# Two GpSimd subtractions made to wait for VectorE's in a tuned attention and mixture kernel

## The chip, the cores and the metric

The kernel runs on one core of a Trainium2 chip. The metric is the device time of one execution in microseconds (us), the median of three runs. Engines are called as the profile calls them: PE is TensorE's matmul, PEld its weight load, DVE is VectorE, ACT is ScalarE, POOL is GpSimd, SP is SyncE.

## What is computed

Attention with a sliding window of 128 positions, then a mixture of four two-layer experts that are all applied to every token, in float32:

```python
# attention: B, H, S, D = 4, 8, 576, 64
scores = q @ k.T / sqrt(D) - slope[h] * (i - j)       # only 0 <= i - j < 128
attn   = softmax(scores) @ v
# experts: N = 2304 tokens, D = 512, E = 4, F = 1024
p = domain_probs / (domain_probs.sum(-1, keepdims=True) + 1e-09)
for e in range(E):
    h = np.maximum(x @ w1[e], 0.0)
    out += p[:, e:e + 1] * (h @ w2[e])
```

## The kernel before

Every float32 operand of a matmul is split into a high part (a cast to the PE's rounded type) and a low part (the operand minus its high part), and a product takes three matmuls: high by high, high by low, low by high. So wherever a matrix is made, a cast (mostly ACT, L338) and a subtraction (DVE or POOL, `minus`, L355) come behind it. On POOL a subtraction or sum over 384 columns or more is cut in two pieces (`pieces`, L346), which leaves two instructions.

The Python program doesn't write its instructions down in a fixed order. It collects operations (`Plan.op`, L55) with the engines that can run them, what they read and write, and a due time. `Plan.order` (L88) then goes forward in estimated time, and at each step takes for an engine the ready operation with the earliest due time. It keeps an account called `port`, which lets no two operations of DVE and POOL that carry that mark overlap in its own estimate. The instructions go out in the order of their planned starts. What keeps the engines apart on the chip are semaphores for true data dependencies alone: the account of `port` leaves no trace in the program.

The last 200 us of the span are six "pairs" (`pair`, L1329). A pair takes two slices of 256 hidden features of one expert together with the last 768 tokens, and multiplies in Strassen's manner with seven products in place of eight, in both layers. Its first layer is products `("a", 0..6)` and `("b", 0..6)` (L1236), its second the seven products of `multiply` (L1459; matmuls at L1469), whose results DVE weights and adds to the accumulators (`weighted`, L1487; instructions at L1488). The left operands of four of the second layer's products are sums of first-layer results, called S1 to S4. Each exists for fi = 0 and 1. For S2 and S3, for example:

- the raw S3 is made by DVE into a tile `q` (L1384), the raw S2 by `plus` from it into a tile `w1r` (L1431, instructions at L1090), the raw S4 by `plus` from that into a tile `q` (L1432, instructions at L1090)
- `split(i, fi)` (L1396) makes the high part on ACT (L338) and the low part by `minus` (L360). For S1 and S2 the subtraction may only go to DVE; in the trace these are the rows `xl<-w1r,xh`. For S3 and S4 it may go to either engine; S3's are on POOL in the trace, `rl<-q,rh`, two pieces of 128x192 for each fi.

The products of one pair that use S2 (`2`), S3 (`3`), "22" and S4 (`4`) are worked off between the first-layer products of the next pair, in the order a0, 2 (tiles 0 and 1), a1, 2 (tile 2), a2, 3 (tiles 0 and 1), and so on (L1339). Product 2 adds to the PSUM bank that product 11 of its own pair has just filled, so its first matmul has to wait until DVE has read that bank at L1488.

Before, L1433 to L1436 read:

```python
                split(3, fi)
                if fi:
                    split(2, 0)
                    split(2, 1)
```

Of the kernel before, what the change touches and what calls it, by code (L numbers as in the profile page):

```python
# [12 lines left out]
ALU = mybir.AluOpType  # L13
# [4 lines left out]
PE, DVE, ACT, POOL, SP = "PE", "DVE", "ACT", "POOL", "SP"  # L18


def f(ap):
    return ap.bitcast(F32)
# [13 lines left out]


class Op:
    __slots__ = ("n", "engs", "emit", "due", "deps", "outs", "wait", "ready", "bufs", "cold", "start", "end", "eng", "port", "late", "lag")


class Plan:
# [9 lines left out]
    def __init__(self):  # L52
        self.ops, self.last, self.readers, self.places = [], {}, {}, {}

    def op(self, engs, emit, due, reads=(), writes=(), holds=(), cold=None, port=None, late=0.0, lag=0.0):  # L55

        o = Op()
        o.n, o.engs, o.emit, o.due = len(self.ops), dict(engs), emit, due
        o.deps, o.outs, o.bufs, o.start = set(), [], [], None


        o.port, o.late, o.lag = (POOL,) if port is None else port, late, lag
        o.cold = 2 * o.engs.get(PE, 0.0) if cold is None else cold
        for key in reads:
            if key in self.last:
                o.deps.add(self.last[key])
        for key in writes:
            if key in self.last:
                o.deps.add(self.last[key])
            o.deps.update(self.readers.get(key, ()))  # L70
        o.deps.discard(o)
        for key in reads:
            self.readers.setdefault(key, []).append(o)
        for key in writes:
            self.last[key] = o
            self.readers[key] = []
        for key in (*reads, *writes, *holds):
            b = key[0] if isinstance(key, tuple) else key
            b = getattr(b, "buf", b)
            if isinstance(b, Buf) and b not in o.bufs:  # L80
                o.bufs.append(b)
                b.uses += 1
        for d in o.deps:
            d.outs.append(o)
        self.ops.append(o)
        return o
# [153 lines left out]
def key_of(b):  # L240
    return b.key if isinstance(b, Part) else b
# [3 lines left out]
def attention_moe(  # L245
# [28 lines left out]
    plan = Plan()  # L274
# [47 lines left out]
    after = sb.tile([P, 2, P], F32, tag="after", name="after")  # L322
# [5 lines left out]
    by = {DVE: nc.vector, POOL: nc.gpsimd}  # L328
# [4 lines left out]
    def cast(o, i, n, due, reads, writes, sbuf=True):  # L333


        def emit(e):
            if e == ACT:
                nc.scalar.activation(o(), i(), AF.Copy)  # L338
            else:
                nc.vector.tensor_copy(o(), i())  # L340

        plan.op(
            {ACT: act(n) + (0.035 if sbuf else 0.0), DVE: dve2(n) if sbuf else dve(n)}, emit, due, reads, writes, port=(DVE,) if sbuf else ()
        )

    def pieces(e, n, *aps):  # L346

        if e != POOL or n < WHOLE:
            return [aps]
        axis = next((i for i in range(1, len(aps[0].shape) - 1) if aps[0].shape[i] % 2 == 0), len(aps[0].shape) - 1)  # L350
        m = aps[0].shape[axis] // 2
        at_ = (slice(None),) * axis
        return [[x[(*at_, slice(i * m, i * m + m))] for x in aps] for i in range(2)]

    def minus(o, a, b, n, due, reads, writes, gp=True):  # L355


        def emit(e):
            for x, y, z in pieces(e, n, o(), a(), b()):
                by[e].tensor_tensor(out=x, in0=y, in1=f(z), op=ALU.subtract)  # L360

        engs = {DVE: dve(n), POOL: pooled(n)} if gp else {DVE: dve(n)}
        plan.op(engs, emit, due, reads, writes, port=(DVE, POOL) if gp else ())

    a, b = EARLY
# [10 lines left out]
    for us, nbs in passes:  # L378
        for u in us:
# [3 lines left out]
            if max(nbs) <= PAIRED and u % 2 == 0 and u + 1 in us:  # L383
                half_of[l], half_of[l + 1] = 0, 1
                for nb in nbs:
                    n = BLOCKS[nb][1]
# [26 lines left out]
            for nb in nbs:  # L413
                n = BLOCKS[nb][1]
# [20 lines left out]
    end = opened[5]  # L435
    if SEVEN[3, 4] < NU:
        end = next(now for l, nb, now in steps if nb == (3, 4)) - AHEAD
# [39 lines left out]
    def segment(g):  # L477
# [59 lines left out]
        if g.plain:  # L537
            return
        cast(lambda: g.kh[:, :, :kn], lambda: k[:, :, :kn], 2 * kn, due, [k], [g.kh])
        cast(lambda: g.qs[:, :, :n], lambda: q[:, :, :n], 2 * n, due, [q], [g.qs])  # L540
        minus(
            lambda: g.qs[hi64, :, :n],
            lambda: q[hi64, :, :n],
# [4 lines left out]
            [g.qs],  # L548
        )
        minus(  # L550
            lambda: g.kl[:, :, :kn],
            lambda: k[:, :, :kn],
# [7 lines left out]
        due += 3  # L560
        cast(lambda: g.vs[:, :vn, 0:4:3, :], v4, 128 * vn, due, [v], [(g.vs, 0)])
        minus(
            lambda: g.vs[:, :vn, 1:3, :],
            v4,
# [449 lines left out]
    def after_group(n0):  # L1014
        for o in plan.ops[n0:]:
            for d in gate:
                if d not in o.deps:
                    o.deps.add(d)
                    d.outs.append(o)
# [67 lines left out]
    def plus(o, a, b, n, due, reads, writes, op=ALU.add):  # L1087
        def emit(e):
            for x, y, z in pieces(e, n, o(), a(), b()):
                by[e].tensor_tensor(out=x, in0=y, in1=z, op=op)  # L1090

        plan.op({DVE: dve(n), POOL: pooled(n)}, emit, due, reads, writes, port=(DVE, POOL))
# [236 lines left out]
    def pair(l0, l1, due, between):  # L1329
# [3 lines left out]
        n = BLOCKS[nbs[0]][1]  # L1333
# [11 lines left out]
        ready, t_ = {}, clock[0]  # L1345
        for x in order:
            x = x if isinstance(x, tuple) else (None, x.__defaults__[-1])
# [20 lines left out]
        for fi in range(2):  # L1368
            h, lo = Buf("rh"), Buf("rl")
# [8 lines left out]
        def relu(o, src, reads, k_, d):  # L1378
            plan.op({ACT: act(n)}, lambda e: nc.scalar.activation(o(), src(), AF.Relu), d, reads, [k_])

        def joined(o, src, b, op, reads, k_, d, sbuf):
            plan.op(
                {DVE: dve(n)},
                lambda e: nc.vector.scalar_tensor_tensor(out=o(), in0=src(), scalar=0.0, in1=f(b()), op0=ALU.max, op1=op),  # L1384
                d,
                reads,
                [k_],
                port=(DVE,) if sbuf else None,
            )

        def halves(name, fi, src, keys, d, sbuf, free=()):
            h, lo, hk, lk = R[name, fi]
            relu(h, src, [*keys, *free], hk, d)
            joined(lo, src, h, ALU.subtract, [*keys, hk], lk, d, sbuf)

        def split(i, fi):  # L1396
            h, lo, hk, lk = S[i, fi]
            r_, rk = s_raw(i, fi), s_key(i, fi)
            n0 = len(plan.ops)
            cast(h, r_, n, ready[i], [rk], [hk])  # L1400
            minus(lo, r_, h, n, ready[i], [rk, hk], [lk], i > 2)
            if i < 3:
                after_group(n0)

# [12 lines left out]
        def result1(src, keys, fi, b):  # L1417
            d = clock[0] - URGENT
            if b == 0:
                h, lo = (Part(t, lambda t: t[:, fi, n : 2 * n], ("r", fi)) for t in (xh, xl))  # L1420
                R["11", fi] = (lambda: h[:, :n]), (lambda: lo[:, :n]), key_of(h), key_of(lo)
                hold.append((src, keys, fi, d))
            else:
                joined(s_raw(1, fi), src, raw(a22, fi), add, [*keys, key(a22, fi)], s_key(1, fi), d - 3, fi == 1)
                relu(raw(a21, fi), src, keys, key(a21, fi), d)
                split(1, fi)
            if len(hold) == 1 and (b == 1) == (fi == 0):
                src, keys, fi, d = hold.pop()
                halves("11", fi, src, keys, d, False, free)
                joined(s_raw(3, fi), src, raw(a21, fi), sub, [*keys, key(a21, fi)], s_key(3, fi), d, False)  # L1430
                plus(s_raw(2, fi), s_raw(3, fi), raw(a22, fi), n, ready[2] - 0.5, [key(a22, fi), s_key(3, fi)], [s_key(2, fi)], sub)  # L1431
                plus(s_raw(4, fi), raw(a12, fi), s_raw(2, fi), n, ready[4] - 0.5, [key(a12, fi), s_key(2, fi)], [s_key(4, fi)])  # L1432
                split(3, fi)  # L1433
                if fi:
                    split(2, 0)
                    split(2, 1)  # L1436

        spare = Buf("av")
        s0, at0, _ = sevenfold(l0, due, result0, Part(spare, lambda t: t.place[0], 0))
# [193 lines left out]
    for i in range(FILL):  # L1633
# [5 lines left out]
            out=after,  # L1639
# [19 lines left out]
            out=dps, in0=dps, scalar1=1.0e-9, scalar2=None, op0=ALU.add  # L1659
# [9 lines left out]
            out=prob, in0=dp, in1=dps[:, :, None].to_broadcast([P, NT // P, E]), op=ALU.mult  # L1669
# [18 lines left out]
    outs = []  # L1688
    for l, nb, due in [*steps, (None, None, now)]:
# [35 lines left out]
        if l is not None:  # L1725
            outs = [] if l in pairs else [(l, b, i) for b in (nb if l in joint else [nb]) for i in range(BLOCKS[b][1] // P)]

    with tc.manual_schedule():
        for o in plan.order():
            o.emit(o.eng)  # L1730


MARGIN = 15.32
# [65 lines left out]
```

## Time and profile before

| | us |
|---|---|
| median of three runs | 911.28 (911.26 to 913.27) |
| the profiled execution, its own time | 911.12 |
| its span in the trace | 909.1 |
| PE busy | 883.8 (97%) |
| DVE busy | 739.5 (81%) |
| POOL busy | 462.0 (51%) |

The profile covers one execution. An engine's line of a timeline gives the start, the duration, and in square brackets how long the engine had been idle and what released it. A duration runs from the start of an instruction on its engine to its end, and so holds any time in which it stood still there. "x3" merges neighbours of one kind into one row, which then runs from the first start to the last end. Times in the trace count from the start of the span.

### The profile page before, as it was taken

The page shows a single profiled execution, that of the slowest core. Times are in us where ns is not written, and L with a number is a line of the kernel's source. Part 1 is how long each engine was busy: PE and PEld are TensorE (multiplying, and loading weights), DVE is VectorE, ACT ScalarE, POOL GpSimd, SP SyncE. Part 2 cuts the span into 40 slices and gives each one's busy share as a digit, 9 for nine tenths or more (in the row PEclk, how much of TensorE's full clock was granted, in tenths as well). Part 3 has the DMA queues.
Part 4 walks back from the last instruction along what each step waited for, and adds up shares of the span by engine and source line. Part 5 has one row for each costly group of instructions (what it writes and reads, how often), then busy time and mean ns, then how long its engine had stood idle before and what let it go on. Part 6 is the DMA issues. An engine that isn't in the chain of part 4 may idle for free.

```text
span 909.1 us, 15674 instructions
## 1 busy us (share of the span) xinstructions
PE 883.8 (97%) x5466; PEld 816.2 (90%) x5466; DVE 739.5 (81%) x1605; ACT 474.6 (52%) x1221; POOL 462.0 (51%) x595
## 2 busy tenths in 40 slices
PE   8999999999999999999999999999999898998997
PEld 5899999999999999999998989899998898998997
DVE  6989879888887889886998878778665879879877
ACT  6877456565677678663443534334242533543542
POOL 4787555556457678763672213218314415535524
PEclk9999999999999999999999999999999999999999
DMA  7766554242445456432366464642333533533602
GB/s 239 228 199 194 170 169 134 86 153 85 136 164 157 141 179 217 139 120 65 128 242 245 163 218 148 215 150 76 110 96 137 186 105 112 201 105 111 203 1 70
DMA packets 47999, 136.19 MB, mean 150 GB/s; under 512 B 4656, under 2 KB 19760, under 8 KB 44848
## 3 DMA queue, kind: packets, MB, share of 16 engines
q1 hardware_dynamic: 43696, 113.17, 37.7%
q0 software_dynamic: 4224, 22.02, 7.2%
q8 instruction: 43, 0.70, 0.3%
q14 instruction: 36, 0.29, 0.1%
HBM read 106.86 MB, written 28.31 MB: 149 GB/s over the span
## 4 chain that ended last, share of the span: by engine, by line
PE 84%; DVE 10%; DMA 2%; ACT 2%; issue 1%; SPq 1%; DVEq 0%; ACTq 0%
PE b L1564 29%; PE b L1158 19%; PE b L1236 18%; PE b L1469 8%; PE av L819 4%; PE b L609 3%; DVE acc L1488 2%; PE b L746 2%; DMA w2r<-in_w 1%; DVE acc L1582 1%; PE av L1469 1%; DVE xl L360 1%; DVE w2l L360 1%; PE av L1236 1%; DMA q<-in_q 1%
## 5 line engine op out<-in xcount | busy, mean ns | idle before, releaser
L1158 PE MATMUL b<-xh,w 128*128 128x256 f32 (+1 forms) x928 | 205.2, 296 | 1.0 <-DVE xh L340 1.0
L1158 PEld LDWEIGHTS b<-xh,w 128*128 128x128 f32 x928 | 156.5, 190 | 3.3 <-DVE xh L340 1.2
L1582 DVE SCALAR_TENSOR_TENSOR acc<-b,prob,acc 128x512 f32<-128x512 f32 x150 | 111.6, 745 | 36.4 <-PE b L1564 35.5
L1564 PE MATMUL b<-w2h,rh 128*128 128x512 f32 x342 | 135.7, 397 | 0.0
L1158 PE MATMUL b<-xl,w 128*128 128x256 f32 (+1 forms) x464 | 135.4, 292 | 0.1
L1564 PE MATMUL b<-w2l,rh 128*128 128x512 f32 x342 | 134.6, 394 | 0.0
L1564 PE MATMUL b<-w2h,rl 128*128 128x512 f32 x342 | 134.4, 393 | 0.0
L782 POOL TENSOR_SCALAR_AFFINE_SELECT pt<-s 128x512 fp32r<-128x512 f32 x120 | 77.3, 669 | 74.5 <-DVE s L360 61.4
L1158 PEld LDWEIGHTS b<-xl,w 128*128 128x128 f32 x464 | 88.0, 190 | 2.4 <-DVE xl L360 0.3
L1564 PEld LDWEIGHTS b<-w2h,rl 128*128 128x128 f32 x342 | 64.2, 188 | 14.7 <-DVE rl L1186 0.4
L690 ACT ACTIVATE s<-s,t 128x128 f32<-128x128 f32 x128 | 50.4, 395 | 50.9 <-DVE t L672 50.3
L360 DVE TENSOR_TENSOR w2l<-w2r,w2h 128x512 fp32r<-128x512 f32 x85 | 76.6, 924 | 0.4 <-ACT w2h L338 0.4
L1179 ACT ACTIVATE rh<-b 128x256 fp32r<-128x256 f32 (+1 forms) x116 | 45.5, 393 | 57.5 <-PE b L1158 55.5
L360 POOL TENSOR_TENSOR w<-w1r,w 128x256 fp32r<-128x256 f32 x74 | 64.5, 896 | 19.9 <-ACT w L338 12.6
L1564 PEld LDWEIGHTS b<-w2h,rh 128*128 128x128 f32 x342 | 64.5, 189 | 8.2
L1249 ACT ACTIVATE s<-b 128x384 f32<-128x384 f32 x81 | 39.6, 489 | 61.7 <-PE b L1236 61.5
L1564 PEld LDWEIGHTS b<-w2l,rh 128*128 128x128 f32 x342 | 64.5, 189 | 7.9
L1186 DVE SCALAR_TENSOR_TENSOR rl<-b,rh 128x256 fp32r<-128x256 f32 (+1 forms) x116 | 51.2, 441 | 25.0 <-ACT rh L1179 24.3
L360 POOL TENSOR_TENSOR w2l<-w2r,w2h 128x256 fp32r<-128x256 f32 x46 | 39.0, 868 | 51.4 <-ACT w2h L338 35.7
L1488 DVE SCALAR_TENSOR_TENSOR acc<-b,prob,acc 128x256 f32<-128x256 f32 x108 | 46.6, 474 | 12.7 <-PE b L1469 12.4
L1236 PE MATMUL b<-xh,w 128*128 128x384 f32 x192 | 56.9, 337 | 0.0
L338 ACT ACTIVATE w2h<-w2r 128x512 fp32r<-128x512 f32 x95 | 56.1, 619 | 1.3 <-PE b L1564 1.1
(223 smaller groups left out, 2415.2 us busy)
## 6 DMA issues: line engine op xcount, KB each, us to landing
w2r<-in_w SPq DMA_DIRECT2D x60, 512.0 KB, 3.6
w1r<-in_w SPq DMA_DIRECT2D x48, 512.0 KB, 4.5
parked<-w SPq DMA_DIRECT2D x12, 1024.0 KB, 5.5
w<-parked POOLq DMA_DIRECT2D x12, 1024.0 KB, 6.0
q<-in_q SPq DMA_DIRECT2D x16, 384.0 KB, 3.4
k<-in_k SPq DMA_DIRECT2D x12, 512.0 KB, 4.5
k<-in_k SPq DMA_DIRECT2D x12, 384.0 KB, 4.4
parked<-pt SPq DMA_DIRECT2D x6, 768.0 KB, 3.3
```

Source lines behind the costliest of these rows:

```text
L338: nc.scalar.activation(o(), i(), AF.Copy)
L360: by[e].tensor_tensor(out=x, in0=y, in1=f(z), op=ALU.subtract)
L690: return lambda e: nc.scalar.activation(sv()[:, h, -m:], sv()[:, h, -m:], AF.Exp, bias=t[:, h : h + 1], scale=-1.0, accum_out=t[:, 2 + h : ...
L782: return lambda e: nc.gpsimd.affine_select(out=pt[:, :, :, c0 + own * P : c0 + own * P + P], in_=hl(), pattern=[[0, 4], [1, P] if own else ...
L1158: nc.tensor.matmul(bk[:, :n], a[0][:, kt, fs], b[:, kt, cols], start=kt == 0 and i == 0, stop=kt == KT - 1 and i == 2,)
L1179: lambda e: nc.scalar.activation(h[:, :n], bk[:, :n], AF.Relu),
L1186: lambda e: nc.vector.scalar_tensor_tensor(out=lo[:, :n], in0=bk[:, :n], scalar=0.0, in1=f(h[:, :n]), op0=ALU.max, op1=ALU.subtract,),
L1236: nc.tensor.matmul(bank[:, :n], x(k), y(k), start=new and k == 0 and i == 0, stop=k == 1 and i == 2, skip_group_check=True,)
L1469: nc.tensor.matmul(bank[bk][part]()[:, cs], a()[:, ns], b()[:, fi, :], start=new and i != 1 and fi == 0 and j == 0, stop=fi == 1 and j == ...
L1488: nc.vector.scalar_tensor_tensor(out=ac[:, ds], in0=bank[bk][part]()[:, cs], scalar=prob[:, nt, e_ : e_ + 1], in1=ac[:, ds], op0=ALU.mult, ...
L1564: nc.tensor.matmul(bk[:, cs], a[:, ns], b[1][:, fi, cs], start=half != 1 and fi == 0 and j == 0, stop=half != 0 and fi == 1 and j == 2, sk ...
L1582: nc.vector.scalar_tensor_tensor(out=o, in0=i_, scalar=p, in1=o, op0=ALU.mult, op1=ALU.add)
```

## The change

The subtraction that makes the low part of S3 (fi) is declared to depend on the subtraction that makes the low part of S2 (same fi). The dependency enters the plan as one more predecessor. Where the two land on different engines, it also enters the program as a semaphore wait, from the last instruction of S2's subtraction to the first of S3's. There are 12 such waits, two for each of the six pairs. No instruction of an engine's arithmetic is added or removed. The calls of `split` for S3 move behind those for S2.

```diff
-    def op(self, engs, emit, due, reads=(), writes=(), holds=(), cold=None, port=None, late=0.0, lag=0.0):
+    def op(self, engs, emit, due, reads=(), writes=(), holds=(), cold=None, port=None, late=0.0, lag=0.0, after=()):
...
+        o.after, o.made = list(after), None
+        o.deps.update(after)
...
-    def minus(o, a, b, n, due, reads, writes, gp=True):
+    def minus(o, a, b, n, due, reads, writes, gp=True, after=()):
         def emit(e):
-            for x, y, z in pieces(e, n, o(), a(), b()):
-                by[e].tensor_tensor(out=x, in0=y, in1=f(z), op=ALU.subtract)
+            return [
+                by[e].tensor_tensor(out=x, in0=y, in1=f(z), op=ALU.subtract) for x, y, z in pieces(e, n, o(), a(), b())
+            ]
...
+        first_ = {}
+
         def split(i, fi):
...
-            minus(lo, r_, h, n, ready[i], [rk, hk], [lk], i > 2)
+            first_[i, fi] = minus(lo, r_, h, n, ready[i], [rk, hk], [lk], i > 2, [first_[2, fi]] if i == 3 else ())
...
-                split(3, fi)
                 if fi:
-                    split(2, 0)
-                    split(2, 1)
+                    for i in (2, 3):
+                        split(i, 0)
+                        split(i, 1)
...
     with tc.manual_schedule():
+        behind = mybir.DependencyInfo(mybir.DependencyClass.Sync, mybir.DependencyReason.DATA)
         for o in plan.order():
-            o.emit(o.eng)
+            o.made = o.emit(o.eng)
+            for d in o.after:
+                if d.eng != o.eng:
+                    tc.add_manual_dep(o.made[0].ins, d.made[-1].ins.name, behind, reason="port")
```

## Rows read from the trace of the kernel before

**Rows 1.** Waits of PE: who waited for whom, total us, times, longest us

```profile
PE b L1469 <- DVE acc L1488: 14.1, 7, 2.7
```

**Rows 2.** Timeline of PE: matmuls that follow an idle stretch, from 690 us on

```profile
692.48 1.34 PE L1236 MATMUL b<-pt,w 128*128 128x384 f32 x6 [0.93 <-DVE x L1316]
...
728.40 0.36 PE L1469 MATMUL b<-w2h,xh 128*128 128x256 f32 x1 [2.44 <-DVE acc L1488]
...
762.52 0.36 PE L1469 MATMUL b<-w2h,xh 128*128 128x256 f32 x1 [2.67 <-DVE acc L1488]
...
895.96 0.36 PE L1469 MATMUL b<-w2h,xh 128*128 128x256 f32 x1 [0.74 <-DVE acc L1488]
```

**Rows 3.** Stretches: busy PE, PEld, DVE, ACT, POOL, granted clock, DMA share, GB/s

```profile
690.00:693.00 3.00, 2.07 (x10) 1.47 (x10) 2.24 (x5) 1.04 (x3) 2.03 (x4) 1.00 0.00 0
...
796.00:797.00 1.00, 0.38 (x3) 0.41 (x4) 1.00 (x4) 0.00 (x0) 0.00 (x0) 1.00 0.00 0
...
798.00:799.00 1.00, 1.00 (x6) 1.00 (x6) 1.00 (x2) 0.00 (x0) 0.00 (x0) 0.50 0.00 0
...
801.00:802.00 1.00, 1.00 (x9) 1.00 (x9) 0.38 (x1) 1.00 (x3) 0.00 (x0) 1.00 0.00 0
```

**Rows 4.** Chain that ended last, second pair: start us, us, what

```profile
754.47 4.32 PE b L1469 x36
758.79 1.06 PE b L1236 x6
...
761.59 0.80 DVE acc L1488 x2
762.38 0.14 issue
762.52 2.42 PE b L1469 x12
764.94 1.82 PE b L1236 x6
...
768.52 1.43 PE b L1469 x12
```

**Rows 5.** Timeline of DVE, second pair

```profile
755.70 4.24 DVE L360 TENSOR_TENSOR xl<-w1r,xh 128x384 fp32r<-128x384 f32 x1
759.87 1.26 DVE L1488 SCALAR_TENSOR_TENSOR acc<-b,prob,acc 128x256 f32<-128x256 f32 x3
761.04 0.54 DVE L360 TENSOR_TENSOR xl<-w1r,xh 128x384 fp32r<-128x384 f32 x1
```

**Rows 6.** Timeline of POOL, second pair

```profile
754.72 1.17 POOL L1090 TENSOR_TENSOR w1r<-q,k 128x192 f32<-128x192 f32 x2
755.85 2.29 POOL L360 TENSOR_TENSOR rl<-q,rh 128x192 fp32r<-128x192 f32 x4
758.11 1.42 POOL L360 TENSOR_TENSOR w2l<-w2r,w2h 128x256 fp32r<-128x256 f32 x2
```

**Rows 7.** Timeline of ACT, second pair

```profile
755.92 0.53 ACT L338 ACTIVATE xh<-w1r 128x384 fp32r<-128x384 f32 x1 [0.90 <-POOL w1r L1090]
756.35 0.62 ACT L338 ACTIVATE w2h<-w2r 128x512 fp32r<-128x512 f32 x1
```

**Rows 8.** Timelines of DVE and POOL, first pair

```profile
721.99 2.77 DVE L1090 TENSOR_TENSOR w1r<-q,k 128x384 f32<-128x384 f32 x1
...
715.97 0.57 POOL L999 DMA_DIRECT2D pt<-parked  x1 [0.20 <-DVE xl L1384]
...
720.93 2.29 POOL L360 TENSOR_TENSOR rl<-q,rh 128x192 fp32r<-128x192 f32 x4
723.19 1.15 POOL L1090 TENSOR_TENSOR q<-k,w1r 128x192 f32<-128x192 f32 x2
```

**Rows 9.** Timelines of DVE and POOL, last pair

```profile
894.13 0.90 DVE L360 TENSOR_TENSOR xl<-w1r,xh 128x384 fp32r<-128x384 f32 x1
...
894.57 0.92 POOL L360 TENSOR_TENSOR rl<-q,rh 128x192 fp32r<-128x192 f32 x1
```

More of the change, by code (lines that the diff above doesn't have):

```diff
@@ L38 @@
 class Op:
-    __slots__ = ("n", "engs", "emit", "due", "deps", "outs", "wait", "ready", "bufs", "cold", "start", "end", "eng", "port", "late", "lag")
+    __slots__ = ("n", "engs", "emit", "due", "deps", "outs", "wait", "ready", "bufs", "cold", "start", "end", "eng", "port", "late", "lag", "after", "made")
 class Plan:
@@ L353, in pieces @@
         return [[x[(*at_, slice(i * m, i * m + m))] for x in aps] for i in range(2)]
-    def minus(o, a, b, n, due, reads, writes, gp=True):
+    def minus(o, a, b, n, due, reads, writes, gp=True, after=()):
         def emit(e):
-            for x, y, z in pieces(e, n, o(), a(), b()):
-                by[e].tensor_tensor(out=x, in0=y, in1=f(z), op=ALU.subtract)
+            return [
+                by[e].tensor_tensor(out=x, in0=y, in1=f(z), op=ALU.subtract) for x, y, z in pieces(e, n, o(), a(), b())
+            ]
         engs = {DVE: dve(n), POOL: pooled(n)} if gp else {DVE: dve(n)}
-        plan.op(engs, emit, due, reads, writes, port=(DVE, POOL) if gp else ())
+        return plan.op(engs, emit, due, reads, writes, port=(DVE, POOL) if gp else (), after=after)
     a, b = EARLY
```

## The prediction, on record before the run

> **What bounds the kernel now.** TensorE (PE) is busy nearly all the time, so the first view to read is PE's list of waits, to see what is left: its longest entry is 14.1 us in 7 waits of the second-layer matmuls (L1469) for DVE's reading of the bank at L1488 [rows 1]. The second view, PE's timeline, places them: all lie in the six pairs, each ahead of product 2. The first pair's wait is 2.44 us, the second's 2.67, the last one's 0.74 [rows 2]; pairs three to five repeat the second to 0.01 us, and a seventh wait of 0.25 us stands near the end, behind the last pair. The third view, the granted clock by stretches, shows what else such a wait costs. In the third pair the clock is still 1.00 (2.4 GHz) when PE starts again, then 0.50 (1.2 GHz) while PE is wholly busy, and 1.00 again some 4 us later; a wait of 0.93 us earlier is followed by no such fall [rows 2, 3]. The chain of work prices the fall: behind the wait of the second pair 12 matmuls of 256 columns take 2.42 us and six of 384 take 1.82, where the same numbers at full clock take 1.43 and 1.06 [rows 4]. That is 2.42 - 1.43 + 1.82 - 1.06 = 1.75 us, in each of the five pairs with a long wait.
>
> **Why DVE is late.** Ahead of the bank's reading, DVE's timeline has S2's subtraction for fi = 0. It takes 4.24 us; its twin for fi = 1, the same shape, takes 0.54 [rows 5]. It starts at 755.70 and ends at 759.94. POOL meanwhile runs without a pause: the end of a sum, S3's four pieces, a weight's two pieces, up to 758.11 + 1.42 = 759.53 [rows 6]. DVE ends 0.41 us after POOL's last piece, about its own working time. In the first pair it is the sum for the raw S2 that stands still: 2.77 us, to 724.76, against POOL's end at 723.19 + 1.15 = 724.34 [rows 8]; again 0.42. So I read these durations as a VectorE instruction that is held for as long as GpSimd keeps issuing instructions that read SBUF.
>
> The Trainium skill, SBUF — State Buffer, section "Who interferes with whom", says that a VectorE instruction with two SBUF inputs contends with a GpSimd instruction that reads SBUF, and that whichever issues first holds the shared pair for that whole instruction. The trace agrees that the two exclude each other. Taken literally the rule speaks against this change: it would let DVE in after one piece. The last pair looks like that: DVE's subtraction takes 0.90 us in the middle of S3's pieces, and the next piece is stretched to 0.92 [rows 9]. The second pair doesn't: six pieces pass DVE by. I go by the second pair, since four of the six are like it; the other reading is a rival below.
>
> **The change, part by part.** No arithmetic is added; 12 waits are, and S3's pieces move back in time. Take the second pair.
>
> 1. S2's subtraction for fi = 0. POOL's sum ends at 754.72 + 1.17 = 755.89 [rows 6]. Next in its queue is S3, which now waits, so DVE is let in and ends at 755.89 + 0.41 = 756.30 instead of 759.94: 3.64 us earlier.
> 2. The three weightings behind it take 1.17 us from start to next start (759.87 to 761.04), so the subtraction for fi = 1 is reached at 757.47 [rows 5]. Its high part is ready by then, at 755.92 + 0.53 = 756.45 [rows 7].
> 3. The wait itself. POOL's nearest row for a release by DVE is 0.20 us [rows 8]; it may be near zero or a few tenths, and it is not on PE's path. S3's first two pieces run from 756.50 for half of 2.29 us, to 757.64. DVE is held for 0.17 us and ends at 757.64 + 0.41 = 758.05. S3's other pieces end at about 758.05 + 0.20 + 1.14 = 759.39, where all four ended at 758.14 before.
> 4. The reading of the bank. PE's 36 matmuls of products 1 and 11 end at 758.79 [rows 4]; the first twelve of product 11's eighteen are done 6/36 of 4.32 = 0.72 us earlier, at 758.07. DVE's two weightings take 0.80 and the release 0.14 [rows 4]; with another 0.14 for PE's own release, product 2 may start at about 758.07 + 0.14 + 0.80 + 0.14 = 759.15. PE is done with a0 at 758.79 + 1.06 = 759.85. So nothing is late: the wait of 2.67 us is gone with 0.7 us to spare, and with it the fall of the clock, since what fell behind 2.67 us didn't fall behind 0.93 [rows 2, 3].
> 5. What is queued behind POOL's wait: S3's later pieces, the weight's two pieces, sums for the next pair, and the issue of its parked weights. S3 is needed by product 3, at 768.52 now and 4.42 earlier in the new order, 764.1; it is there at 759.4 [rows 4]. This delay of 1.25 us costs nothing; without those 4.7 us of cover it would cost itself. The weight's pieces belong to the next pair, which reaches the same place 34.1 us later (728.40 to 762.52 [rows 2]).
>
> So pairs two to five give 2.67 + 1.75 = 4.42 each, 17.7 together. In the first pair 2.77 - 0.54 = 2.23 us of DVE's delay goes and 0.17 may come back at S2's second half: 2.06 of the wait of 2.44 goes, a wait of 0.38 stays, the clock holds, and the gain is 2.06 + 1.75 = 3.8. In the last pair, S2's second subtraction falls from 0.90 to 0.54: 0.4. The sum is 21.9 us, and 911.12 - 21.9 = 889.2 in the profiled execution's terms (span 909.1). The median is 0.16 higher: 889.4. I take 889.6.
>
> Bounds: not a gap could fall further than to nothing. The six waits are 2.44 + 4 x 2.67 + 0.74 = 13.9 and the clock 5 x 1.75 = 8.75, 22.6 in all, so the floor is 888.7, or 888 with the spread of the rows. On the other side the plan is made anew, and I can't see its order in this trace. If POOL's weight pieces (1.42) come in between S3's halves, S2's second half ends at 757.64 + 1.42 + 0.41 = 759.47, product 2 starts at 759.47 + 0.80 + 0.14 = 760.41, and a wait of 0.56 us stays: four pairs, 2.2 us, 891.7 with the clock held. That is still the forecast's case.
>
> **The rivals.**
>
> *Other work of POOL takes S3's place ahead of S2.* POOL is idle at 755.89 in the new order, and the plan may put a ready piece there. The weight's pieces are not ready (their cast begins at 756.35 [rows 7]), but S4's sum is (1.15 us, on POOL in the first pair [rows 8]). One such sum moves step 1 to 757.45 and step 2 to 759.2, and leaves a wait of about 0.3; two leave about 1.5. Whether the clock falls behind 1.5 us no row shows: the gain would be 1.2 to 2.9 in each of four pairs, 911.3 - (4.8 to 11.6) - 4.2 = 895 to 902. For it: the first pair has just such an order. Against it: S2 is due first.
>
> *The wait does nothing.* If the hold ends after one piece, as the skill's rule has it, the 4.24 us have another cause, and DVE is no earlier: 911.3. For it: the last pair. Against it: in all of the five other pairs DVE ends 0.41 to 0.42 behind POOL's last piece.
>
> *The hold moves to S2's second half: slower.* POOL now stops in the middle of S3; whatever the plan puts between the halves holds DVE's subtraction for fi = 1. Today that one starts at 761.04 [rows 5]; a burst of POOL's that ends at 760.6 or later makes it as late, which takes 760.6 - 757.64 = 3.0 us of work between the halves. Two S4 sums, a weight's pieces and a second weight's would be 2 x 1.15 + 2 x 1.42 = 5.1 us, which makes the wait 2.1 us longer than today: 5 x 2.1 = 10.7, 922. Against it: S2's due time lies before all of these, and only one weight is ready then.
>
> **How the numbers follow.** The forecast, 888 to 892: 0.68. Other work ahead of S2, 892 to 902: 0.18. The wait does nothing, or what it gives is lost: 0.08, within 0.3% of 911.3 (2.7 us, about what a measurement of this kernel can tell from no change). Slower: 0.06. A range from 887.8 to 900 leaves out the last two and a few of the second case. Faster by over 0.3%: 0.86; within: 0.08; slower: 0.06.
>
> **What would show it.** In the changed kernel's timeline S2's first subtraction should take under 1 us in every pair and end before the first `rl<-q,rh` starts; S2's second should stand before the third of these pieces; PE's waits at L1469 for L1488 should be under 1 us in all, and the clock 1.00 from the first pair to the last; a pair should last 29.7 us from product 2 to product 2, not 34.1. The prediction is wrong if a `TENSOR_TENSOR` of DVE of 2 us or more is left ahead of product 2, if the clock falls behind a shorter wait, or if PE waits at product 3 for S3.

## The result: 890.45 us, and the profile after

The changed kernel takes 890.45 us (median of four runs, 890.15 to 892.15) against 912.14 for the kernel before in runs of the same time (911.26 to 913.27): a ratio of 0.9764, with a 95% interval of 0.9749 to 0.9778. Forecast were 889.6. The profiled execution takes 890.15 with a span of 888.3. Medians here and below are over all executions of a kernel, and the ratios leave out the few at a lowered clock (one of the kernel with small issues, one of the first kernel that joins both cures, one of the kernel before).

PE's list of waits (total, times, longest) against [rows 1]: 14.1 us for DVE's reading of the bank have become 1.0. The line numbers have moved by two to four; L1492 is the former L1488, L1473 the former L1469. With the first pair's 0.63 us, which the list puts down to ACT but which are DVE's too (see below), it is 1.6.

```profile
PE b L1473 <- DVE acc L1492: 1.0, 2, 0.7
```

PE's timeline from 690 us on shows the idle stretches against [rows 2]. Between the first pair's product 2 and the last pair's there is none; the first pair keeps 0.63, the last one 0.74.

```profile
692.83 1.31 PE L1238 MATMUL b<-pt,w 128*128 128x384 f32 x6 [1.48 <-DVE x L1318]
...
716.65 1.32 PE L1238 MATMUL b<-pt,w 128*128 128x384 f32 x6 [0.65 <-DVE x L1318]
...
726.94 0.35 PE L1473 MATMUL b<-w2h,xh 128*128 128x256 f32 x1 [0.63 <-ACT s L1251]
...
875.18 0.36 PE L1473 MATMUL b<-w2h,xh 128*128 128x256 f32 x1 [0.74 <-DVE acc L1492]
```

The first pair's wait is DVE's, although the bracket names ACT's copy at L1251. Two weightings (`acc<-b,prob,acc`) take 0.86 us, so the bank is read at 725.93 + 0.86 = 726.79, and product 2 starts 0.15 us later, as it does behind DVE in the kernel before (0.14 in [rows 4]). ACT's copy ends at 726.83, but in the second pair product 2 is under way (756.84) before that copy has even begun (756.88), so it doesn't wait for it. DVE is late because S3's second half runs on DVE in the first pair, between S2's second subtraction and the weightings:

```profile
724.91 1.09 DVE L361 TENSOR_TENSOR rl<-q,rh 128x384 fp32r<-128x384 f32 x1
725.93 1.25 DVE L1492 SCALAR_TENSOR_TENSOR acc<-b,prob,acc 128x256 f32<-128x256 f32 x3
```

The stretches of the same kernel (columns as in [rows 3]) show PE wholly busy and the clock at 1.00 through pairs two to five:

```profile
750.00:780.00 30.00, 30.00 (x215) 30.00 (x214) 26.26 (x53) 15.02 (x32) 17.31 (x25) 1.00 0.47 160
...
840.00:870.00 30.00, 30.00 (x215) 30.00 (x215) 26.16 (x53) 15.02 (x32) 15.48 (x23) 1.00 0.15 54
```

And the chain of work has product 2 in the second pair right behind a0, at 756.84, its 12 matmuls in 1.43 us and the six behind them in 1.04, where [rows 4] have 2.42 and 1.82. In the first pair, behind the 0.63 us, the 12 take 1.68:

```profile
726.94 1.68 PE b L1473 x12
...
755.80 1.04 PE b L1238 x6
756.84 1.43 PE b L1473 x12
758.27 1.04 PE b L1238 x6
```

The timelines of DVE and POOL in the second pair answer to [rows 5, 6]:

```profile
752.72 0.62 DVE L361 TENSOR_TENSOR xl<-w1r,xh 128x384 fp32r<-128x384 f32 x1
...
754.43 0.63 DVE L361 TENSOR_TENSOR xl<-w1r,xh 128x384 fp32r<-128x384 f32 x1
```

```profile
751.15 0.57 POOL L1001 DMA_DIRECT2D w<-parked  x1
751.73 1.18 POOL L1092 TENSOR_TENSOR w1r<-q,k 128x192 f32<-128x192 f32 x2
753.48 1.17 POOL L361 TENSOR_TENSOR rl<-q,rh 128x192 fp32r<-128x192 f32 x2 [0.57 <-ACT xh L340]
754.61 1.48 POOL L1092 TENSOR_TENSOR q<-k,w1r 128x192 f32<-128x192 f32 x2
756.04 1.62 POOL L361 TENSOR_TENSOR rl<-q,rh 128x192 fp32r<-128x192 f32 x2
```

S2's first subtraction has fallen from 4.24 to 0.62 us. S3's first half now starts 0.57 us behind the sum, when DVE is through. (The bracket names an ACT cast; in the instructions' semaphores that first piece waits for DVE too, so this is a wait for two, put down to one of them. DVE ends at 753.34.) The order of PE, ACT and SP is the same in both kernels, instruction for instruction. That of POOL isn't. In pairs two to five one of S4's two sums `q<-k,w1r` has moved from DVE to POOL, in between S3's halves, and a weight's pieces have gone to DVE in its place. In the first pair S4's sum runs ahead of S3, and S3's second half runs on DVE; in the last pair one S4 sum has moved in between S3's halves. So the program has 11 of these waits, not 12.

### The profile page after: what moved, and what is told of

It reads as the page before. It is cut to its first block, busy times and chain, and to the rows that moved or that the text cites. A ratio compares the mean times of both kernels' runs of the same rounds, so it can differ in the third digit from the quotient of the medians.

```text
span 888.3 us, 15672 instructions
## 1 busy us (share of the span) xinstructions
PE 875.1 (99%) x5466; PEld 808.6 (91%) x5466; DVE 726.9 (82%) x1605; ACT 474.0 (53%) x1221; POOL 465.9 (52%) x595
## 4 chain that ended last, share of the span: by engine, by line
PE 85%; DVE 10%; ACT 2%; DMA 1%; issue 1%; DVEq 0%; ACTq 0%; SPq 0%
PE b L1568 29%; PE b L1160 19%; PE b L1238 18%; PE b L1473 8%; PE av L821 4%; PE b L611 3%; PE b L748 2%; DMA w2r<-in_w 1%; DVE acc L1586 1%; PE av L1473 1%; DVE w2l L361 1%; PE av L1238 1%; DVE xl L361 1%; DVE acc L1492 1%; DVE b L1257 1%
## 5 line engine op out<-in xcount | busy, mean ns | idle before, releaser
L361 DVE TENSOR_TENSOR w2l<-w2r,w2h 128x512 fp32r<-128x512 f32 x88 | 79.4, 925 | 0.4 <-ACT w2h L340 0.4
L1251 ACT ACTIVATE s<-b 128x384 f32<-128x384 f32 x81 | 39.5, 488 | 53.7 <-PE b L1238 53.5
L361 POOL TENSOR_TENSOR w2l<-w2r,w2h 128x256 fp32r<-128x256 f32 x40 | 35.4, 906 | 51.4 <-ACT w2h L340 35.7
L361 DVE TENSOR_TENSOR w<-w1r,w 128x512 fp32r<-128x512 f32 x59 | 50.7, 879 | 0.1
```

The lines of the kernel that those rows point to most:

```text
L1251: {ACT: act(n)}, lambda e: nc.scalar.activation(pv(p), bank[:, :n], AF.Copy), at[0] - URGENT, [bank], [p]
```

## The experiments

The theories: (1) the semaphore counts, since DVE is held while POOL goes on issuing instructions that read SBUF; (2) the new order of POOL's and DVE's work counts, and the semaphores are idle; (3) each instruction of POOL's holds DVE at most once, and DVE is let in behind it, which was a rival of the prediction. A fourth, A, came up in the second set. By a run of POOL's the text means instructions of POOL that follow each other without a pause; a pause shows as a bracket in its timeline.

### The order without the semaphores

```diff
-            for d in o.after:
-                if d.eng != o.eng:
-                    tc.add_manual_dep(o.made[0].ins, d.made[-1].ins.name, behind, reason="port")
```

> The order of the changed kernel (the dependency stays in the plan), without the 11 semaphore waits. Theory 1 (the semaphore is what counts: VectorE's subtraction for S2, fi 0, is held while GpSimd goes on issuing reading instructions): behind the sum that ends at 752.9 come S3 (1.14 us), S4's sum (1.14) and S3's second half (1.14), to 756.3; the subtraction ends at 756.3 + 0.41 = 756.7, product 2 starts at 756.7 + 1.17 + 0.47 + 0.80 + 0.14 = 759.3 instead of 756.84, a wait of 2.4 us with the fall of the clock in each of pairs two to five, about 908 to 911 us. Theory 2 (the new order of GpSimd's and VectorE's work is what counts): 890.5.

Measured: 908.18 us (906.41 to 908.59), 0.9965 of the kernel before (0.9951 to 0.998). DVE's timeline, POOL's and PE's in the second pair:

```profile
754.38 3.97 DVE L361 TENSOR_TENSOR xl<-w1r,xh 128x384 fp32r<-128x384 f32 x1
```

```profile
756.77 1.16 POOL L361 TENSOR_TENSOR rl<-q,rh 128x192 fp32r<-128x192 f32 x2
```

```profile
728.61 0.36 PE L1473 MATMUL b<-w2h,xh 128*128 128x256 f32 x1 [1.89 <-DVE acc L1492]
...
760.92 0.49 PE L1473 MATMUL b<-w2h,xh 128*128 128x256 f32 x1 [2.40 <-DVE acc L1492]
```

DVE ends at 754.38 + 3.97 = 758.35, 0.42 behind POOL's last piece (757.93), and PE waits the 2.40 us that were worked out. The semaphores carry most of the gain; theory 2 falls. The new order is worth the rest, some 3 us: 0.27 us of wait in each of four pairs, and in the first pair 0.55 us and the clock, which holds behind 1.89.

### The semaphores without the order

The kernel before, with a wait of S3's subtraction for S2's wherever S2's goes out first in its own order. That is 6 waits: fi = 0 in pairs two to five, both in the last pair. (In this expectation the rivals have other numbers: its theory 2 is (3) of the list above, its theory 3 is (2).)

```diff
+                    for x in range(2):
+                        first_[3, x].after = [first_[2, x]]      # not in o.deps: no part of the plan
...
+            for d in o.after:
+                if d.eng != o.eng:
+                    if d.made is None:
+                        continue
+                    tc.add_manual_dep(o.made[0].ins, d.made[-1].ins.name, behind, reason="port")
```

> The order of the kernel before, with the semaphore waits alone, wherever S2's subtraction goes out ahead of S3's in that order: fi 0 in pairs two to five and both in the last pair, 6 waits; none in the first pair, and none for fi 1 in pairs two to five. Theory 1 (held until GpSimd's burst ends): S2 fi 0 ends at 756.3, S3 and a weight run from 756.5 for 2.29 + 1.42 us to 760.2, S2 fi 1 asks at 757.5 and ends at 760.6, product 2 starts at 761.5: waits of 1.7 us in place of 2.67, 907 us, or 900 if the clock holds behind 1.7. Theory 2 (VectorE is let in behind the running instruction, as the page on SBUF has it): fi 1 ends at 758.1, no wait in pairs two to five, 893.6. Theory 3 (the order counts): 911.

Measured: 893.82 us (891.69 to 895.62), 0.9804 (0.9778 to 0.9831). Pairs two to five have no wait of PE left; the first pair, which has no semaphore, keeps 2.42 us. S2's second subtraction on DVE, and POOL, in the second pair:

```profile
757.97 0.63 DVE L361 TENSOR_TENSOR xl<-w1r,xh 128x384 fp32r<-128x384 f32 x1
```

```profile
757.01 2.61 POOL L361 TENSOR_TENSOR rl<-q,rh 128x192 fp32r<-128x192 f32 x4 [0.57 <-ACT xh L339]
```

This is where theory 1 in its plain form fails. The second subtraction comes in the middle of POOL's unbroken run of S3 and the weight, and is let in after one piece: 0.63 us, and POOL's four pieces take 2.61 in place of 2.29. The same two kinds of instruction meet in the kernel before, and DVE is held for 4.24. Something about the run other than its length decides: it goes on for 3.4 us behind the start of this subtraction, and for 3.8 in the kernel before.

### One half of the semaphores at a time

In the changed kernel, only the waits for fi = 0, then only those for fi = 1:

```diff
-                if d.eng != o.eng:
+                if d.eng != o.eng and o.fi == 0:      # the other kernel: o.fi == 1
```

> The changed kernel without the waits for fi 1 (6 waits stay, fi 0). Theory 1 in its strict form (held through any unbroken burst): S2 fi 1 asks at 754.5 and is held until S4's sum and S3's second half are through, 753.5 + 3.4 = 756.9, ends at 757.3, product 2 starts at 758.3, a wait of 1.4 us in four pairs, 896 us or more with the clock. As the trace of the changed kernel has it (fi 1 is let in between S3's second piece and S4's sum, with no wait there): 890.5, and the second six waits give nothing.

> The changed kernel without the waits for fi 0 (the waits for fi 1 stay). Theory 1: S2 fi 0 asks at 752.8 and is held through S3's first half and S4's sum until GpSimd stops at its wait for fi 1, at 752.9 + 2.3 = 755.2; it ends at 755.6, product 2 starts at 755.6 + 1.17 + 0.47 + 0.80 + 0.14 = 758.2 instead of 756.84: a wait of 1.4 us in four pairs, 896 us, or 903 if the clock falls behind 1.4. If it is let in behind the running instruction: 890.5.

Measured: 890.14 us (889.95 to 892.29) with the waits for fi = 0 alone, as good as the change; 899.5 (897.2 to 901.36) with those for fi = 1 alone. In the second kernel DVE is held until POOL stops at its own wait for fi = 1. DVE, POOL, PE:

```profile
753.61 2.85 DVE L361 TENSOR_TENSOR xl<-w1r,xh 128x384 fp32r<-128x384 f32 x1
```

```profile
754.88 1.15 POOL L1092 TENSOR_TENSOR q<-k,w1r 128x192 f32<-128x192 f32 x2
...
758.17 1.14 POOL L361 TENSOR_TENSOR rl<-q,rh 128x192 fp32r<-128x192 f32 x2 [2.14 <-DVE xl L361]
```

```profile
759.03 0.35 PE L1474 MATMUL b<-w2h,xh 128*128 128x256 f32 x1 [1.29 <-DVE acc L1493]
```

753.61 + 2.85 = 756.46, 0.43 behind the end of S4's sum at 756.03. So the six waits for fi = 0 are the change; the other five give nothing, because the second subtraction is let in anyhow.

### A memset between the pieces; the pieces twice

The kernel before, once with a memset ahead of each of S3's pieces, once with each piece computed a second time into a spare tile:

```diff
+                if pause and e == POOL:
+                    nc.gpsimd.memset(spare_, 0.0)                 # 128 x 16
                 by[e].tensor_tensor(out=x, in0=y, in1=f(z), op=ALU.subtract)
```

```diff
                 by[e].tensor_tensor(out=x, in0=y, in1=f(z), op=ALU.subtract)
+                if twice is not None and e == POOL:
+                    by[e].tensor_tensor(out=spare_[2 * twice + j], in0=y, in1=f(z), op=ALU.subtract)
```

> The kernel before, with a small GpSimd memset of a spare tile, which reads no SBUF, ahead of each of S3's pieces (48 half-pieces of the pairs less those on VectorE; no wait on VectorE). If the hold ends wherever GpSimd has an instruction that reads no SBUF, S2's first subtraction gets in at the first memset, at about 756.3 in the second pair, and its second at another: no long waits, 890 to 894 us. If it is held until GpSimd's queue stops, the burst is longer by four memsets: 911.4 or slightly more.

> The kernel before, with each of S3's pieces on GpSimd computed a second time into a spare tile: GpSimd's burst ahead of product 2 is 2.29 us longer in each pair, and nobody reads the copy. Theory 1 (VectorE is held to the end of the burst): S2's first subtraction takes 4.24 + 2.29 = 6.5 us in pairs two to five, the first pair's sum 2.77 + 2.29 = 5.1, product 2 comes 2.3 us later in five pairs, 911.4 + 11.5 = 922.9. If each reading instruction holds VectorE once at most: 911.4.

Measured: 911.98 us (1.0016, 1.0004 to 1.0029) and 927.6 (1.0189, 1.0174 to 1.0204). DVE's subtraction in the second pair, first with the memsets, then with the doubled pieces:

```profile
757.71 4.41 DVE L364 TENSOR_TENSOR xl<-w1r,xh 128x384 fp32r<-128x384 f32 x1
```

```profile
759.68 6.41 DVE L362 TENSOR_TENSOR xl<-w1r,xh 128x384 fp32r<-128x384 f32 x1
```

An instruction that reads nothing, of 0.10 us, doesn't end the hold. Twice the pieces make it 2.17 us longer, nearly the 2.29 that were added: in these two kernels DVE is held to the end of POOL's run. The time grew by more than the 11.5 us expected, by 16.4. The wait is 4.85 us in the second pair, and its clock is at 1.2 GHz before PE starts again and for longer after, as the chain shows: 12, 6, 6 and 6 matmuls take 2.90, 1.92, 1.28 and 1.15 us in place of the 1.43, 1.04, 0.71 and 1.04 that the changed kernel's chain has for the same steps, 3.0 us of loss in place of 1.75.

```profile
768.67 2.90 PE b L1473 x12
771.56 1.92 PE b L1240 x6
773.48 1.28 PE b L1473 x6
774.76 1.15 PE b L1240 x6
```

### The same kernel without GpSimd's DMA issues

What the held instructions had in common: since its last pause, POOL had issued a load of parked weights (L999), as at 751.15 above. That gave theory A. The expectation says that the run "began with such an issue"; in the second pair of the kernel before, the issue stands in the middle of the run. That pair shows both cases. Ahead of the issue, DVE's subtraction is let in behind the running piece (0.67 us), and POOL's next two pieces are stretched to 1.75, where two of this size take 1.42 in [rows 6]. Behind it, six pieces pass DVE by [rows 5, 6].

```profile
752.21 0.67 DVE L360 TENSOR_TENSOR xl<-w1r,xh 128x384 fp32r<-128x384 f32 x1
```

```profile
752.43 1.75 POOL L360 TENSOR_TENSOR xl<-w2r,xh 128x256 fp32r<-128x256 f32 x2
754.13 0.57 POOL L999 DMA_DIRECT2D w<-parked  x1
```

The kernel before, with these loads issued by SyncE, and nothing else changed:

```diff
-                lambda e, o=o, i=i: nc.gpsimd.dma_start(out=o(), in_=i[:]),
+                lambda e, o=o, i=i: nc.sync.dma_start(out=f(o()), in_=i[:]),
```

> The kernel before, with the loads of the parked weights issued by SyncE in place of GpSimd; no wait is added. In the traces so far every long hold of VectorE (4.24, 3.97, 2.85, 2.77 us) lies in a run of GpSimd's that began with such an issue, and every subtraction that was let in after one piece (0.6 to 0.9 us) lies in a run that began otherwise. Theory A (the issue is what makes the hold last): S2's first subtraction is let in after one piece, under 1 us in all pairs, waits at product 2 under 1 us, 890 to 895 us. Theory B (any unbroken run holds it): GpSimd's run ends 0.57 us earlier for want of the issue, the wait is 2.1 us, 901 to 909 us.

Measured: 889.17 us (888.83 to 890.1), 0.9768 (0.9753 to 0.9782), a little less than theory A expected. There is no wait of S3 for S2 in this kernel. DVE and POOL in the second pair:

```profile
752.60 0.91 DVE L360 TENSOR_TENSOR xl<-w1r,xh 128x384 fp32r<-128x384 f32 x1
...
754.61 0.90 DVE L360 TENSOR_TENSOR xl<-w1r,xh 128x384 fp32r<-128x384 f32 x1
```

```profile
751.04 1.49 POOL L1090 TENSOR_TENSOR w1r<-q,k 128x192 f32<-128x192 f32 x2
752.49 2.60 POOL L360 TENSOR_TENSOR rl<-q,rh 128x192 fp32r<-128x192 f32 x4
755.05 1.75 POOL L360 TENSOR_TENSOR w2l<-w2r,w2h 128x256 fp32r<-128x256 f32 x2
```

The same run of POOL, sum, four pieces, weight, without a pause, now lets DVE in twice after one piece each (0.91 and 0.90 us), and is itself stretched by 0.3 us each time. All of the gain is there without the change. One hold goes that the change leaves in place: in the first pair `w1r<-x,k` takes 1.78 us on DVE, before (716.65) and after (716.98), up to 0.42 behind the end of two pieces of POOL that follow an issue; here it takes 0.55, and a wait of PE of 0.55 us that hangs on it (720.94 before, 721.27 after) is gone.

### A small issue, and a memset, in its place

In that kernel, next to each load on SyncE, GpSimd issues a small one of 128 x 16 numbers, or runs a memset of 128 x 512:

```diff
+                lambda e, o=o, i=i, x=x: (nc.sync.dma_start(out=f(o()), in_=i[:]), nc.gpsimd.dma_start(out=tiny, in_=i[:, 0, :16])),
```

```diff
+                lambda e, o=o, i=i, x=x: (nc.sync.dma_start(out=f(o()), in_=i[:]), nc.gpsimd.memset(tiny, 0.0)),
```

> The parked loads on SyncE, and in the place of each of GpSimd's issues a small one: 128 x 16 numbers into a spare tile. Theory A (an issue at the head of GpSimd's run makes VectorE's hold last, whatever its size): S2's first subtraction takes about 4.2 us again in pairs two to five, 908 to 911 us. If it is the large transfer's own work that does it: under 1 us, 889 to 890. The last pair has no such issue in any of these kernels and should stay at 0.9 us.

> The parked loads on SyncE, and in the place of each of GpSimd's issues a memset of a spare tile of 128 x 512, which occupies GpSimd about as long (0.6 us) and reads nothing. Theory A (it is the issue): S2's first subtraction stays under 1 us, 889 to 890.5 us. Theory C (any instruction at the head that gives GpSimd's queue time to fill makes the hold last): 4.2 us, 908 to 911.

Measured: 907.46 us with the small issue (0.9966, 0.994 to 0.9992), 889.96 with the memset (0.9768, 0.9747 to 0.9789). POOL and DVE in the second pair of the kernel with the small issue:

```profile
750.95 0.55 POOL L1001 DMA_DIRECT2D tiny<-parked  x1
...
754.89 1.42 POOL L360 TENSOR_TENSOR w2l<-w2r,w2h 128x256 fp32r<-128x256 f32 x2
```

```profile
752.53 4.21 DVE L360 TENSOR_TENSOR xl<-w1r,xh 128x384 fp32r<-128x384 f32 x1
```

and with the memset:

```profile
750.59 0.52 POOL L1001 MEMSET tiny<- 128x512 f32 x1
```

```profile
752.16 0.54 DVE L360 TENSOR_TENSOR xl<-w1r,xh 128x384 fp32r<-128x384 f32 x1
...
753.81 0.92 DVE L360 TENSOR_TENSOR xl<-w1r,xh 128x384 fp32r<-128x384 f32 x1
```

With a small issue in the run, DVE is held to the run's end again in pairs two to five: 752.53 + 4.21 = 756.74, 0.43 behind 754.89 + 1.42 = 756.31. With a memset of the same length there, the first subtraction isn't held at all and the second is let in after one piece. The last pair, which has no issue in any of these kernels, has 0.92 and 0.90 us for the two subtractions in the first of the two kernels as in the second. So it isn't the size of the transfer, nor the time that an instruction in that place gives GpSimd's queue to fill.

The first pair of the kernel with the small issue doesn't fit. An issue stands right ahead of S3's four pieces, which follow without a pause, and yet DVE's sum is let in after one piece, at 0.86 us, where the kernel before has 2.77 [rows 8]:

```profile
719.98 0.55 POOL L1001 DMA_DIRECT2D tiny<-parked  x1 [0.78 <-DMA tiny<-parked]
720.55 3.00 POOL L360 TENSOR_TENSOR rl<-q,rh 128x192 fp32r<-128x192 f32 x4
```

```profile
720.80 0.86 DVE L1092 TENSOR_TENSOR w1r<-q,k 128x384 f32<-128x384 f32 x1
```

Theory A is right, then, in that every long hold of these traces has an issue ahead of it in POOL's run. It isn't shown that an issue is always enough. PE's wait in that first pair is 1.68 us and its clock holds, which is part of why this kernel takes less than the 908 us expected.

### What is left: S4's sum, and the two cures together

The changed kernel, with S4's sum made to wait as well; then that kernel with the parked loads on SyncE too:

```diff
-                plus(s_raw(4, fi), raw(a12, fi), s_raw(2, fi), n, ...)
...
+                    for x in range(2):
+                        plus(s_raw(4, x), raw(a12, x), s_raw(2, x), n, ..., after=[first_[2, x]])
```

> The changed kernel, with the sum for the raw S4 made to wait as well, for S2's subtraction of the same fi. In the last pair S4's sums stretch both of S2's subtractions to 0.9 us and PE waits 0.74 us at product 2; without them in front it should wait 0.1 or less: 889.8 us against 890.45. Pairs two to five have nothing left to give, so no more than that; if the plan moves S4's sums into the way of VectorE's other work, it is slower than 890.45.

> Three things together: the waits of the change, S4's sum made to wait too, and the parked loads on SyncE. If either cure alone takes nearly all there is (PE is idle for 4 to 5 us in all from 690 us on in either), the sum of them gives only what is left at the first and the last pair: 888.5 to 889.5 us. If the waits cost GpSimd something once VectorE gets in without them, 890 or more.

> The kernel that joins the three once more, to see its time against the same kernel before a second time and its trace: 887.4 to 888.5 us, waits of PE for the reading of the bank (L1492) under 0.7 us in all, S2's subtractions unheld (0.65 us or less) in the last pair too.

Measured: 889.52 us (889.31 to 891.12), where the last pair's wait is 0.35 in place of 0.74 (0.1 or less was expected). The first pair's wait is gone too: both halves of S3 are on POOL there. With the loads on SyncE as well, 887.82, below the 888.5 expected, and, once more against its own runs of the kernel before, 887.37 (887.33 to 887.59), 0.9734 (0.9721 to 0.9747). That is the fastest of these kernels, 3 us below the change. Part of that is the wait of 0.55 us in the first pair, which this kernel doesn't have either. Its list of PE's waits has for the bank:

```profile
PE b L1473 <- DVE acc L1492: 0.6, 2, 0.3
```

## Why the prediction came out right, and where its reason was too wide

By its own steps:

- Step 1, S2's first subtraction: it was to start at once and end 0.60 us after its start (755.70 to 756.30); it takes 0.62. Right.
- Step 2 and 3, its second: 757.47 to 758.05 forecast, 0.58 us; it takes 0.63. POOL's order there is another one than worked out: S4's sum, not S3's second half, stands behind S3's first, and without a pause. That it cost nothing was luck. By the prediction's own reading S4's sum would have held DVE on, to 754.61 + 1.17 + 0.41 = 756.19, and product 2 to 756.19 + 0.80 + 0.14 = 757.13, a wait of about 0.3 us in each of four pairs. Two errors, the order and the reading, cancelled there, for about 1.2 us.
- Step 4, no wait in pairs two to five, no fall of the clock: right. A pair lasts 29.66 us (756.84 to 786.50 in the chain), forecast 29.7.
- Step 5, POOL's delay costs nothing: right. Product 3 follows a2 without a wait.
- The first pair keeps 0.63 us, forecast 0.38. S2's sum came down from 2.77 to 0.55 as forecast, and the 0.17 at S2's second half didn't come. But S3's second half took 1.02 us of DVE's time ahead of the bank's reading, where a weight's subtraction had taken 0.60: 0.42 - 0.17 = 0.25. The clock, too, gives back less than 1.75 while some wait is left: the 12 matmuls behind it take 1.68 us, not 1.43, at a granted clock of 1.00.
- The last pair was to give 0.4 and gave nothing: the wait is 0.74 as before. S2's second subtraction still takes 0.90, because it meets S3's own first half, which has started late behind S4's first sum (the rows are below). With S4's sum waiting too, neither subtraction is held: the two stand back to back, from 871.24 to 872.33, and the wait is 0.35.
- The sum was 889.2 for the profiled execution, and 890.15 were measured. Of the 0.95, 0.48 are the first pair, 0.4 the last, and 0.33 lie ahead of the pairs: the first of them is reached at 716.65 in place of 716.32, behind a wait for L1318 that was 0.93 us before [rows 2] and is 1.48 here. That wait goes from 0.93 to 2.03 in the traces of this case, in code that is the same in all of them, so I take it for scatter. On the other side pairs two to five gave 0.1 more than forecast, and the time outside of the span is 0.17 shorter.
- Of the signs that it named, one failed: PE's waits for the bank were to be under 1 us in all, and they are 1.6 with the first pair's.

The last pair of the changed kernel, POOL and DVE:

```profile
872.66 1.17 POOL L361 TENSOR_TENSOR rl<-q,rh 128x192 fp32r<-128x192 f32 x2
```

```profile
873.34 0.90 DVE L361 TENSOR_TENSOR xl<-w1r,xh 128x384 fp32r<-128x384 f32 x1
```

The step whose reason failed is the one on why DVE is late. The prediction took the hold to last "for as long as GpSimd keeps issuing instructions that read SBUF", went by the five pairs that agreed and left the last pair unexplained. That pair was a clue, and so was the subtraction of 0.67 us ahead of the issue in the second. The hold lasts for the rest of the run only where an issue on GpSimd's queue lies ahead of it in that run; without one, DVE is let in behind the running piece, in the middle of the same run. The Trainium skill, SBUF — State Buffer, section "Who interferes with whom", has the shared pair held for one whole instruction. The kernel with its loads on SyncE agrees with that (0.91, 0.90); the long holds behind an issue don't (4.24, 3.97, 2.85, 6.41, 4.21). The rival with DVE let in after one piece, at 0.08, concluded that the wait does nothing. That conclusion was wrong: what the wait removes is the case that this reading doesn't cover.

The change cures it because POOL stops. The issue stands at 751.15, the sum behind it ends at 752.91, and then POOL waits for DVE. Not only is S2's first subtraction let in there: behind that stop the second one is let in after one piece, with the same issue a little further back, which is why the five waits for fi = 1 are not needed. A memset between the pieces is not such a stop.

What stays open is what in the issue does this, why the first pair of the kernel with the small issue is free of it, and how short a stop would do. No run here tells.

## What to carry to other kernels

When a VectorE instruction with two SBUF inputs takes several times its usual time, lay GpSimd's timeline beside it. In these traces a held instruction ended 0.41 to 0.43 us behind GpSimd's piece, and what had to be found was whether it was the running piece or the last of the run. If it is the last, look for a DMA issue in that run. Moving such issues to another queue is worth a try first; here that alone gave all that the 11 waits gave. Where they must stay, one wait of GpSimd behind the issue, for the VectorE instruction that matters, was enough here.

## What the runs showed of the hardware beyond that

The granted clock after a wait of PE. In the execution without the semaphores it stayed at 1.00 (2.4 GHz) behind a wait of 1.89 us and fell to 0.50 (1.2 GHz) behind one of 2.40, 32 us later. Over all traces it fell behind the waits of 2.38 us and more, with one exception, and it held behind those up to 2.03, with another. A wait of 1.96 us in the kernel with the memsets was followed by a fall, where four other kernels have 2.00 to 2.03 at the same place without one; and a wait of 2.63 in the kernel with the small issue, in its fourth pair, was followed by none. First that of 1.96, then that of 2.63, each with a stretch right behind it:

```profile
692.78 2.16 PE L1240 MATMUL b<-pt,w 128*128 128x384 f32 x6 [1.96 <-DVE x L1320]
```

```profile
693.00:694.00 1.00, 1.00 (x4) 1.00 (x4) 0.69 (x2) 1.00 (x3) 0.11 (x1) 0.50 0.60 86
```

```profile
827.47 0.35 PE L1471 MATMUL b<-w2h,xh 128*128 128x256 f32 x1 [2.63 <-DVE acc L1490]
```

```profile
828.00:829.00 1.00, 1.00 (x11) 1.00 (x10) 1.00 (x3) 0.00 (x0) 0.00 (x0) 1.00 0.00 0
```

So the length of the wait alone doesn't decide; what else does, no run here shows.

A wait that is shortened from 2.67 to 1.29 us, as with the waits for fi = 1 alone, gave back most of the clock's loss as well: behind it 12 and 6 matmuls take 1.68 and 1.04 us, where they took 2.42 and 1.82, which is 1.52 us. In the profiled execution of that kernel, 897.2 us, this makes 4 x (1.38 + 1.52) = 11.6 us, and the first pair, whose wait is 1.92 and whose clock holds, 0.52 + 1.52 = 2.0: 13.6 together, where 911.12 - 897.2 = 13.9 are seen. Its other executions took 898.35 to 901.36 us; no trace shows why.
